# Attention and ELU feed-forward on one Trainium2 core: the first tile's scores put ahead of the global queries' scores and fetched first in pieces, the exponential table loaded at the start, and the weight conversion passes given lower priority while attention runs alone

## The chip, the core and the metric

The kernel runs on 1 core of one Trainium2 chip. The core has five engines with instruction queues of their own: TensorE (PE; its weight loads are shown apart as PEld), VectorE (DVE), ScalarE (ACT), GpSimd (POOL) and SyncE (SP, which issues most DMAs). An engine works off its queue in order, and an instruction waits until what it needs from other engines or from DMAs has been signalled. The metric is the device time of one execution in microseconds (us), lower is better.

## The reference

```python
B, H, Sl, Sg, D = 8, 8, 512, 32, 64
k_all, v_all = concat([k_g, k_l]), concat([v_g, v_l])
out_g = softmax(q_g @ k_all.T / 8) @ v_all            # 32 global queries see everything
s_ll  = where(|i - j| <= 32, q_l @ k_l.T / 8, -1e9)   # local queries see a window ...
out_l = softmax(concat([q_l @ k_g.T / 8, s_ll])) @ v_all   # ... and the 32 global keys
x = concat([out_g, out_l]) as (4608, 512)
h = x @ w_in                                          # 512 -> 2048
out = where(h > 0, h, exp(min(h, 0)) - 1) @ w_out     # 2048 -> 512
```

Inputs and outputs are fp32. The weights arrive with their 64 bits as pairs of 32-bit words (`w_in`, `w_out` are doubles), so the kernel has to turn them into numbers that TensorE can take.

## The kernel before, in words

**Two streams of work share the engines.** One is attention, the other the feed-forward network (FFN). The program is written as Python generators that take turns; a tile framework then orders the instructions of each engine by priority (the place in the program, shifted by `high_priority`), and that order is fixed when the kernel is built.

**Attention** goes through slots. A slot `("g", b, g)` treats the global queries of four heads (batch b, head group g), a slot `("l", b, g, t)` one tile of 128 local queries of four heads. Stage S of a local slot (`stage_s`) computes four score tiles of 128x160 on PE (L769), then DVE adds the mask and takes the row extreme (L780), ACT takes the exponential (L786), DVE adds and inverts the sums (L790, L791, L795), and POOL scales (L793). Stage T transposes the four tiles on PE (L809), and DVE or ACT copies them back (L811). Stage U transposes the global part (L742, L744, L745; copies L746, L748, L750 on ACT, sum L753 on DVE). Stage V multiplies with the values (L853, L822), ACT copies the result (L859), DVE sums and takes the maximum (L864, L866, L868). The global slot (`stage_ga`) has its scores (L703, L706), maxima (L715, L716), exponentials (L720, L722), and `norm` (L726 to L728 on DVE; L731, L732 on POOL). Slots were listed for batch 0 as g, then four l, then g, four l.

**The alone stretch.** For the first 66 steps of attention (`PACE`), `lead[0]` is true: FFN work is not started. Only the weight conversion runs beside attention. `load_weights` works in units: unit 0 is the first 256 columns of `w_in`, unit 1 the matching rows of `w_out`, unit 2 `w_in` again, and so on; two raw buffers (`raw`) alternate, so the fetch of unit 2 (SP, L174) has to wait until unit 0 has read its raw buffer for the last time. The passes of a unit are s0 (absolute value on ACT L188, clamp on POOL L189), s1a, s1b, s1c (three integer passes on DVE: L193, L196, L200), s1d (maximum on ACT, L204, which is the last user of `raw`), s2 (for `w_in` units the maximum over partitions, a PE transpose L141 and a DVE reduction L142), s3 (scale, high half on ACT L213) and s4 (low half on DVE L216). `tables` then makes group scales that the FFN needs.

**FFN.** A block of 256 tokens is split in high and low halves (`split_x`: L568 on ACT, L571 on DVE), multiplied on PE (L324), put through ELU (ACT L333, L334, L335, L349; DVE L342, L345) and multiplied again (L447, later L482 in a form with seven products). In PE's queue the first FFN product stands behind a dozen tiles' attention work.

**Start.** Ten PE products of zeros (`WARM`, L152) run first. The queue of SP begins with the global queries, two k tiles of 640 KB, two q tiles of 256 KB, the mask of 240 KB, then weights and values.

## Time and profile before

| | |
|---|---|
| median of 3 runs | 953.43 us (948.69, 953.43, 953.65) |
| profiled execution | 954.72 us, span of the trace 952.9 us |
| granted TensorE clock, mean | 0.977 |
| PE busy | 908.5 us (95%) |
| DVE busy | 728.1 us (76%) |
| ACT busy | 670.1 us (70%) |
| POOL busy | 271.1 us (28%) |
| first attention score product (L769) starts | 7.89 us |
| first exponential of a score tile (L786) starts | 11.23 us |
| first FFN product (L324) starts | 77.15 us |

Times in the trace count from the span's start. A row of the timeline reads: start, duration, engine, line, operation, what is written and read, the shape, the number of like instructions merged, and in brackets the idle time of that engine before it and what ended it. A row of the windows view gives for one stretch the busy time of each engine, the granted clock of PE, the busy share of the DMA engines and GB/s.

### The profile page before, as it was taken

Reading aid. Unit: us, or ns where it says so; the run is one execution under the profiler, and the core shown is the slowest. Engines: PE = TensorE matmul, PEld = TensorE weight load, DVE = VectorE, ACT = ScalarE, POOL = GpSimd, SP = SyncE. Lnnn points to the kernel's source line nnn. Section 1 sums busy time; section 2 is a strip of 40 time slices with the busy share of each in tenths; the row PEclk is TensorE's granted clock in tenths of the full one; section 3 lists DMA queues with packets and bytes.
Section 4 is the critical chain, followed back from the end, with each engine's and each line's share of the span. In section 5 each row is a group of like instructions: output and inputs, shape, how many; then the busy total and the mean of one; then the engine's idle time right before and its main releaser. Section 6 shows DMA issues by size and latency. Waiting matters only on the chain.

```text
span 952.9 us, 23830 instructions
## 1 busy us (share of the span) xinstructions
PE 908.5 (95%) x9216; PEld 727.8 (76%) x9216; DVE 728.1 (76%) x2025; ACT 670.1 (70%) x1584; POOL 271.1 (28%) x483
## 2 busy tenths in 40 slices
PE   6889887899999999999999999999999999999997
PEld 3567564566666788888888888888888888888886
DVE  4988988889967777768776877687777777676566
ACT  5888996776656767757677767677767767666564
POOL 4655481461522322122121212221332312100000
PEclk8779999899999999999999999999999999999999
DMA  6855876331342023101330123102310101000000
GB/s 262 299 179 180 282 224 191 124 123 57 115 157 90 23 100 103 47 26 46 105 121 26 46 78 125 47 27 79 122 49 25 46 23 35 2 23 23 1 24 23
DMA packets 41769, 87.64 MB, mean 92 GB/s; under 512 B 7736, under 2 KB 8888, under 8 KB 41656
## 3 DMA queue, kind: packets, MB, share of 16 engines
q1 hardware_dynamic: 41368, 85.85, 26.6%
q8 instruction: 73, 1.20, 0.5%
q14 instruction: 40, 0.33, 0.1%
q10 hardware_dynamic: 288, 0.26, 0.1%
HBM read 70.89 MB, written 15.20 MB: 90 GB/s over the span
## 4 chain that ended last, share of the span: by engine, by line
PE 67%; DVE 14%; ACT 9%; POOL 3%; issue 3%; DMA 3%; SPq 0%; DVEq 0%; ACTq 0%; POOLq 0%
PE pa L324 25%; PE acc L482 12%; PE h L482 9%; PE acc L447 4%; PE pa L822 3%; PE h L324 3%; PE pa L769 3%; PE pa L809 2%; ACT p L786 2%; DMA raw<-w_out 2%; PE pa L889 2%; DVE gl L345 1%; POOL p L793 1%; DVE cu L196 1%; DVE cu L200 1%
## 5 line engine op out<-in xcount | busy, mean ns | idle before, releaser
L324 PEld LDWEIGHTS <-winh 128*128 128x128 f16 x2160 | 209.4, 98 | 39.2 <-issue 8.4
L793 POOL TENSOR_SCALAR p<-p,sm 128x128 f32<-128x128 f32 x256 | 147.8, 593 | 303.2 <-DVE sm L791 165.0
L324 PE MATMUL pa<-xh,winh 128*128 128x256 f16 x824 | 224.9, 273 | 0.1
L324 PE MATMUL pa<-xl,winh 128*128 128x256 f16 x824 | 224.6, 273 | 0.0
L324 PE MATMUL pa<-xh,winl 128*128 128x256 f16 x824 | 224.6, 273 | 0.0
L361 ACT ACTIVATE gh<-gx,xs 128x896 f16<-128x896 f32 x103 | 107.3, 1042 | 123.1 <-DVE gx L358 123.0
L345 DVE SCALAR_TENSOR_TENSOR gl<-gx,xs,gh 128x896 f16<-128x896 f32 x103 | 119.4, 1159 | 59.9 <-ACT gh L361 59.0
L482 PEld LDWEIGHTS <-gh 128*128 128x128 f16 x1456 | 139.5, 98 | 24.0 <-issue 7.4
L786 ACT ACTIVATE p<-p,m 128x160 f32<-128x160 f32 x256 | 106.7, 421 | 41.6 <-DVE m L780 41.4
L324 PEld LDWEIGHTS <-winl 128*128 128x128 f16 x1080 | 106.1, 98 | 14.3 <-issue 1.2
L333 ACT ACTIVATE g<-pa,xs 128x512 f32<-128x512 f32 x103 | 70.3, 682 | 24.4 <-PE pa L324 23.8
L482 PE MATMUL acc<-wouth,gh 128*128 128x256 f16 x312 | 85.2, 273 | 0.0
L482 PE MATMUL acc<-woutl,gh 128*128 128x256 f16 x312 | 85.1, 273 | 0.0
L335 ACT ACTIVATE g<-g 128x512 f32<-128x512 f32 x135 | 85.0, 630 | 0.1
L482 PE MATMUL acc<-wouth,gl 128*128 128x256 f16 x312 | 85.0, 273 | 0.0
L482 PEld LDWEIGHTS <-gl 128*128 128x128 f16 x728 | 71.2, 98 | 9.2 <-DVE gl L345 1.0
L482 PE MATMUL h<-raw,gh 128*128 128x256 f16 x416 | 75.0, 273 | 0.0
L324 PE MATMUL h<-xh,winh 128*128 128x256 f16 x256 | 71.1, 279 | 1.5 <-ACT hs L334 0.9
L324 PE MATMUL h<-xl,winh 128*128 128x256 f16 x256 | 71.0, 278 | 0.7 <-DVE xl L571 0.7
L324 PE MATMUL h<-xh,winl 128*128 128x256 f16 x256 | 71.0, 278 | 0.0
L780 DVE CUSTOM_DVE_ANT_0 p<-pa,msk 128x160 f32<-128x160 f32 x228 | 61.5, 318 | 4.8 <-PE pa L769 4.7
L342 DVE SCALAR_TENSOR_TENSOR gx<-g,hs 128x512 f32<-128x512 f32 x51 | 35.9, 704 | 36.0 <-ACT g L335 35.6
(236 smaller groups left out, 2016.9 us busy)
## 6 DMA issues: line engine op xcount, KB each, us to landing
k<-kT SPq DMA_DIRECT2D x32, 640.0 KB, 5.1
v<-vT SPq DMA_DIRECT2D x64, 256.0 KB, 2.8
q<-qT SPq DMA_DIRECT2D x32, 256.0 KB, 5.6
raw<-w_in SPq DMA_DIRECT2D x8, 1024.0 KB, 5.9
raw<-w_out SPq DMA_DIRECT2D x8, 1024.0 KB, 6.8
out<-o SPq DMA_DIRECT2D x32, 256.0 KB, 2.3
od<-o SPq DMA_DIRECT2D x24, 256.0 KB, 3.1
o<-od SPq DMA_DIRECT2D x24, 256.0 KB, 2.8
```

The source lines that it names most:

```text
L324: nc.tensor.matmul(h[:, j, :], wt[:, c, f], xt[:, c, :], start=k == 0, stop=k == 11)
L333: nc.scalar.activation(g, hf, AF.Relu, scale=sc[:, p:p + 1])
L335: nc.scalar.activation(g, g, AF.Exp, scale=-1.0)
L342: nc.vector.scalar_tensor_tensor(out=out, in0=ins[0], scalar=-1.0, in1=ins[1], op0=ALU.add, op1=ALU.max)
L345: nc.vector.scalar_tensor_tensor(out=dst, in0=src, scalar=sg, in1=hi, op0=ALU.mult, op1=ALU.subtract)
L361: nc.scalar.activation(gh, gx, AF.Copy, scale=sg)
L447: nc.tensor.matmul(acc[t], gt[:, s], wt[:, f, :], start=p == first and j == 0 and k == 0, stop=p == last and j == 1 and k == 2)
L482: nc.tensor.matmul(cols, gt, w, start=p == 0 and k == 0, stop=last and k == len(todo) - 1, skip_group_check=True)
L769: nc.tensor.matmul(sp[r][half * HQ:(half + 1) * HQ, j * KW:(j + 1) * KW], q[rows, qs], k[rows, t, half, :], start=True, stop=True)
L780: nc.vector.tensor_tensor_reduce(out=p, in0=sp[r][:, j * KW:(j + 1) * KW], in1=msk[:, mi, :], op0=ALU.add, op1=ALU.min, scale=-scale, scal ...
L786: nc.scalar.activation(ps[i], ps[i], AF.Exp, bias=m[:, i:i + 1], scale=-1.0, accum_out=s[:, 0, i:i + 1])
L793: nc.gpsimd.tensor_scalar(ps[i][:, 0:P], ps[i][:, 0:P], s[:, 1, i:i + 1], 1.0, ALU.mult, ALU.mult)
```

## The change

Seven edits, all in the start and the alone stretch:

1. The slots of batch 0 begin with the first local tile; the first global slot comes second.
2. `first_loads` replaces the two calls of `loads`: SP fetches the keys of tile 0 (`k[:, 0]`, 160 KB each), ACT's queue the queries of tile 0 (64 KB each), SP the first third of the mask (80 KB), then the global queries, the rest of k, the rest of q, the rest of the mask.
3. A tile `early` of one column is set to zero and put through `Exp` at the start.
4. `WARM` goes from 10 to 8.
5. In the alone stretch the passes s1a, s1b, s1c, s1d, s3 and s4 of a unit get a priority 60 places lower (`behind`); s0 and s2 keep theirs.
6. `behind` moves from `add_up` to the top, unchanged.
7. The mask is no longer fetched in `loads`.

```diff
-WARM = 10
+WARM = 8
...
+    def behind(fn):
+        with tc.high_priority(offset=-BEHIND):
+            fn()
...
+    early = wts.tile([P, 1], F32, name="early")
+    nc.vector.memset(early, 0.0)
+    nc.scalar.activation(early, early, AF.Exp)
...
-            defer(i, fn)
+            defer(i, (lambda fn=fn: behind(fn)) if lead[0] and fn not in (s0, s2) else fn)
...
-                slots += [(*a, *t) for g in range(2) for a, t in [(("g", b, g), ())] + [(("l", b, g), (t,)) for t in range(NT)]]
+                slots += [("l", b, 0, 0), ("g", b, 0)] + [("l", b, 0, t) for t in range(1, NT)]
+                slots += [("g", b, 1)] + [("l", b, 1, t) for t in range(NT)]
...
-                if i == 1:
-                    nc.sync.dma_start(msk, mask)
-
-        for i in range(AHEAD):
-            loads(i)
+
+        def first_loads():
+
+            st = sts[0]
+            for hp in range(2):
+                k = st["k", hp] = apool.tile([P, NT, 2, KW], F32, name="k", bufs=4)
+                q = st["q", hp] = apool.tile([P, SL], F32, name="q", bufs=4)
+                nc.sync.dma_start(k[:, 0], kT[0, hp][:, 0])
+                nc.scalar.dma_start(q[:, 0:P], qT[0, hp][:, 0:P])
+            nc.sync.dma_start(msk[:, 0, :], mask[:, 0, :])
+            st["qg", 0] = load_qg(0, 0)
+            for hp in range(2):
+                nc.sync.dma_start(st["k", hp][:, 1:], kT[0, hp][:, 1:])
+            for hp in range(2):
+                nc.sync.dma_start(st["q", hp][:, P:], qT[0, hp][:, P:])
+            nc.sync.dma_start(msk[:, 1:, :], mask[:, 1:, :])
+
+        first_loads()
```

How the built queues differ. In the rows of the change line numbers are 3 to 7 higher (L786 is now L789, L188 now L195, L204 now L211, L174 now L181, L780 now L783, L141 now L145, L216 now L223).

ACT, from its first instruction, before (`pg`, `pu` are the global queries' exponentials, `p_94`, `p_95`, `p_93` the score tiles of the first three local tiles, `cu` a conversion unit):

```order
L720 ACT_TABLE_LOAD
L720 ACTIVATE pg,sg<-pa,mg 128x4x64 x2
L722 ACTIVATE pu,sg<-pa,mg 128x32
L786 ACTIVATE p_94,sm<-p_94,m 128x160 x4
L188 ACTIVATE cu<-raw 128x1024
L786 ACTIVATE p_95,sm<-p_95,m 128x160 x4
L786 ACTIVATE p_93,sm<-p_93,m 128x160 x2
L188 ACTIVATE cu<-raw 128x1024
```

and in the change:

```order
L947 DMA q<-qT 128x128 x2
L157 ACT_TABLE_LOAD
L157 ACTIVATE early<-early 128x1
L789 ACTIVATE p_94,sm<-p_94,m 128x160 x4
L723 ACTIVATE pg,sg<-pa,mg 128x4x64 x2
L725 ACTIVATE pu,sg<-pa,mg 128x32
L789 ACTIVATE p_95,sm<-p_95,m 128x160 x4
L789 ACTIVATE p_93,sm<-p_93,m 128x160 x2
L195 ACTIVATE cu<-raw 128x1024
```

The table load stands at the head, the first tile's exponentials ahead of the global ones, and the first absolute value behind ten exponentials where it was behind four.

DVE, around the first tile of the second head group (`p_95` here), before: the three integer passes of unit 2 (L193, L196, L200) stand ahead of its scores.

```order
L193 TENSOR_SCALAR cu<-cu 128x1024
L216 SCALAR_TENSOR_TENSOR winl<-cu,cm,winh 128x4x256
L196 SCALAR_TENSOR_TENSOR cu<-raw,cu 128x1024
L726 TENSOR_REDUCE sg<-sg 128x1
L866 TENSOR_TENSOR xglob<-xglob,h 128x2x32
L200 SCALAR_TENSOR_TENSOR cu<-raw,cu 128x1024
L727 TENSOR_SCALAR sg<-sg 128x1
L868 TENSOR_REDUCE xm<-xr 128x1
L728 RECIPROCAL sg<-sg 128x1
L780 ISA p_95,m<-acc,msk 128x160
```

and in the change, from the same sum of the global queries to the end of that tile's scores and the pass behind them:

```order
L729 TENSOR_REDUCE sg<-sg 128x1
L730 TENSOR_SCALAR sg<-sg 128x1
L731 RECIPROCAL sg<-sg 128x1
L200 TENSOR_SCALAR cu<-cu 128x1024
L223 SCALAR_TENSOR_TENSOR woutl<-cu,cm,wouth 128x1024
L223 SCALAR_TENSOR_TENSOR winl<-cu,cm,winh 128x4x256
L783 ISA p_95,m<-acc,msk 128x160
```

Two of the three integer passes of unit 2 have moved behind this tile's scores; both low halves (L216, now L223) of units 0 and 1 stand right ahead of them.

PE, the second tile's transposes, before and in the change (`cm` is the maximum of weight unit 0):

```order
L822 MATMUL h<-ptw_81,v 64x96 x4
L141 MATMUL pa<-ident,cm 128x128
L809 MATMUL pa<-ident,p_95 128x128 x4
L742 MATMUL pa<-ident,pz 128x128
L745 MATMUL pa<-ident,pg 128x128
```

```order
L825 MATMUL h<-ptw_81,v 64x96 x4
L145 MATMUL pa<-ident,cm 128x128
L812 MATMUL pa<-ident,p_95 128x128 x4
L745 MATMUL pa<-ident,pz 128x128
L748 MATMUL pa<-ident,pg 128x128
```

Nothing moved here: in both, the second tile's transposes stand behind the maximum of unit 0, whose last pass is one of those that got the lower priority.

The queues differ only at their beginning. Line numbers and buffer numbers aside, the last difference stands at place 625 of PE's 12,309 entries, 358 of DVE's 1,997, 156 of ACT's 1,067, 72 of POOL's 242 and 53 of SP's 174.

## The prediction

> **What bounds the kernel now.** First I read the page's slices for PE and its clock, to see where time can be won at all.

> ```profile
> PE   6889887899999999999999999999999999999997
> PEclk8779999899999999999999999999999999999999
> ```

> After the first eight slices (190 us) PE is nine tenths busy or more at full clock. A stretch table by what the change touches says more; its columns are length, then busy time and count for PE, PEld, DVE, ACT, POOL, then clock, DMA share, GB/s.

> ```profile
> 0.00:9.06 9.06, 7.49 (x63) 3.41 (x66) 1.33 (x4) 0.30 (x1) 2.69 (x12) 1.00 0.76 274
> 9.06:22.79 13.73, 6.20 (x53) 3.60 (x48) 9.13 (x41) 11.67 (x40) 6.35 (x12) 0.73 0.71 273
> 22.79:36.97 14.18, 11.89 (x148) 8.53 (x144) 13.03 (x42) 10.40 (x30) 8.11 (x13) 0.90 0.77 269
> 36.97:62.48 25.51, 24.07 (x266) 16.69 (x262) 22.47 (x112) 21.25 (x78) 16.80 (x32) 0.73 0.80 270
> 62.48:77.15 14.67, 11.52 (x124) 8.43 (x117) 11.20 (x48) 10.54 (x37) 10.85 (x31) 0.77 0.27 82
> 77.15:135.00 57.85, 52.73 (x502) 37.32 (x500) 50.83 (x148) 53.76 (x128) 33.61 (x51) 1.00 0.71 241
> 200.00:952.90 752.90, 740.39 (x7701) 615.86 (x7699) 564.44 (x1508) 511.60 (x1177) 166.24 (x295) 1.00 0.18 61
> ```

> From 200 us PE works 740.39 of 752.90 us; nothing there is touched, all queues being the same from about 135 us on. So what is won or lost before is carried to the end, and the question is how much earlier the state at 135 us comes. Until the first FFN product at 77.15 us DVE has the fullest row: idle 7.73, 4.60, 1.15, 3.04 and 3.47 us in the five stretches (length less busy), 20.0 in all. The same DVE work stands ahead of that product before and after (four units up to s1c, four low halves, the same tiles), so its start moves by the idle time that goes or comes. That is my bookkeeping. The waits behind the idle time, from the timelines:

> ```profile
> 1.18 4.21 PE L152 MATMUL acc<-wouth 128*128 128x512 f16 x10 [1.18 <-DVE wouth L150]
> 6.84 0.63 PE L703 MATMUL pa<-k,qg 64*32 64x256 f32 x4 [0.39 <-DMA k<-kT]
> 7.89 0.50 PE L769 MATMUL acc<-k,q 64*64 64x160 f32 x8
> 9.06 0.33 DVE L780 CUSTOM_DVE_ANT_0 p<-acc,msk 128x160 f32<-128x160 f32 x1 [0.38 <-PE acc L769]
> 8.76 1.28 ACT L720 ACT_TABLE_LOAD   x1 [8.76 <-DVE mg L716]
> 10.06 0.47 ACT L720 ACTIVATE pg<-pa,mg 128x256 f32<-128x256 f32 x1
> 11.23 0.43 ACT L786 ACTIVATE p<-p,m 128x160 f32<-128x160 f32 x1
> 11.64 0.42 ACT L786 ACTIVATE p<-p,m 128x160 f32<-128x160 f32 x1
> 12.36 1.37 POOL L731 TENSOR_SCALAR pk<-pu,sg 32x32 f32<-32x32 f32 x4 [8.90 <-ACT p L786]
> 13.82 0.70 POOL L732 TENSOR_SCALAR pg<-pg,sg 128x512 f32<-128x512 f32 x1
> 14.93 1.17 PE L809 MATMUL pa<-ident,p 128*128 128x128 f32 x3 [3.89 <-POOL p L793]
> 16.72 0.69 DVE L193 TENSOR_SCALAR cu<-cu 128x1024 int32<-128x1024 int32 x1 [2.86 <-POOL cu L189]
> 18.77 0.27 ACT L750 COPY ptg<-pa 128x128 f32<-128x128 f32 x1
> 18.83 1.22 DVE L196 SCALAR_TENSOR_TENSOR cu<-raw,cu 128x1024 int32<-128x1024 int32 x1
> 21.53 1.16 ACT L204 ACTIVATE raw<-cu 128x1024 f32<-128x1024 f32 x1 [0.53 <-DVE cu L200]
> 22.42 0.80 PE L853 MATMUL h<-ptg,ptw 128*64 128x160 f32 x4 [2.98 <-DVE ptg L753]
> 22.79 0.38 SPq L174 DMA_DIRECT2D raw<-w_in  x1
> 24.96 0.48 PE L141 MATMUL pa<-ident,cm 128*128 128x128 f32 x1
> 36.97 0.30 DVE L780 CUSTOM_DVE_ANT_0 p<-acc,msk 128x160 f32<-128x160 f32 x1
> ```

> and from the waits of SP's queue (total, times, longest):

> ```profile
> SPq L174 <- ACT raw L204: 22.4, 5, 11.1
> ```

> To be seen: the first exponential of a tile comes at 11.23 us, behind a table load of 1.28 us that waits 8.76 us for the global maxima, and behind the global exponentials. POOL gets its first attention work at 12.36, the transposes start at 14.93, the values only at 22.42. SP holds the third weight fetch, and all loads queued behind it, for 11.1 us until L204 of unit 0 ends, and issues it at 22.79. The second tile's transposes stand behind L141 at 24.96, which waits for the same L204.

> **The change part by part.** *Start.* Eight warm products end at 1.18 + 8 x 0.42 = 4.55 us. The small pieces are 528 KB; at the 274 GB/s of the first stretch that is 1.9 us, and bytes flow from about 2 us on, so they land by about 4. The score products then start at 4.6, and DVE's first score row follows as before by 9.06 - 7.89 = 1.17, at 5.7 us: 3.3 us earlier. The first exponential follows at about 6.0, 5.2 us earlier. The two warm products less cost nothing here: PE would wait for data anyway. The table load lies in ACT's idle 8.76 us, behind two DMA issues like SP's of 0.38 us (from about 0.7: 0.7 + 0.8 + 1.28 = 2.8, well before 6.0). If that cover were gone it would cost the 1.28 us of its row. The memset and the one-column exponential cost DVE and ACT some 0.2 us each, in idle time too.

> The global scores now need the rest of k, fetched third; up to it 1.5 MB have to land, where the second k tile (1.3 MB with the first) landed at 6.84 with 0.75 MB on the way beside it, so about 7 us, and DVE waits for them from 6.2 to 7.7. SP issues nine transfers ahead of the first weights where it issued six, 3 x 0.4 = 1.2 us more; their reader L188 moves back behind ten exponentials (10 x 0.41 us) and starts at about 12.7 as against 12.88, so the later landing stays hidden, narrowly.

> *First tiles.* DVE then does sums of tile 0 and the second tile's scores (to 10.5); POOL scales tile 0 from about 8.8, and the transposes start at 9 (14.93 before). POOL's global scaling (1.37 + 0.70) follows at 11.3 and ends at 13.4; three ACT copies of 0.27 us behind the transposes end at 14.6, and the first values start at 15.0 as against 22.42, 7.4 us earlier. The lowered passes of unit 0 go behind that: clamp on POOL to 15.8, the DVE passes 0.69 + 1.22 + 1.22 us from there to 19.0, with small sums in their overlaps, L204 to about 20.4. So SP's hold opens 2.4 us earlier, and L141 comes at 20.5, 4.4 us earlier. DVE's idle time up to there: 4.8 (start), 1.65 (rest of k), 0.35 and 0.1 (global exponentials), 1.0 (copies), 0.95 (clamp), 8.85 in all, against 12.33 in the first two stretches: **3.5 us won**.

> *Middle.* The order behind gives some of it back. ACT's absolute value of unit 2 now stands between the global exponentials and their last one, so DVE's L726 waits for it. By the same sums over in-order queues I find three DVE waits: 1.4 us at 20 (the clamp of unit 1 stands behind POOL's scaling of the third tile), 2.6 at 27.4 (L726, behind two copies' groups, 1.0 of global exponentials and L188's 1.13 on ACT) and 0.6 at 30 (the clamp of unit 2): 4.6 in all, where the stretch from 22.79 to 36.97 has 1.15, so 3.45 more. The scores of the second head group start near 33.7 (36.97 before), but two passes of 1.22 us that stood ahead of them now follow. I may set POOL and ACT too late, as each is less full than DVE there: I take **2.5 us lost**, between 0 and 3.45. The stretch from 36.97 to 62.48 I leave at its 3.04 us of idle time: lowered passes may fill part of it (up to 3.0 won), and new waits may come.

> *End of the alone stretch.* Here one stall in ACT's queue is moved past.

> ```profile
> 64.60 1.13 ACT L188 ACTIVATE cu<-raw 128x1024 f32<-128x1024 f32 x1 [1.61 <-DMA raw<-w_out]
> 65.63 1.13 ACT L568 ACTIVATE xh<-xr,xm 128x1024 f16<-128x1024 f32 x1
> 66.79 2.14 DVE L571 SCALAR_TENSOR_TENSOR xl<-xr,xm,xh 128x1024 f16<-128x1024 f32 x1 [1.52 <-ACT xh L568]
> 67.82 1.08 PE L809 MATMUL pa<-ident,p 128*128 128x128 f32 x4 [2.41 <-ACT pg L720]
> 70.51 0.80 PE L853 MATMUL h<-ptg,ptw 128*64 128x160 f32 x4
> 73.58 0.23 DVE L864 COPY xglob<-h 128x64 f32<-128x64 f32 x1 [1.51 <-ACT xr L859]
> ```

> L188 waits 1.61 us for weights while L568 and the global exponentials stand behind it; DVE idles 1.52, PE 2.41, its clock falls (0.77 in this stretch), the values at 70.51 take long, and DVE idles another 1.51. In the change's queue L568 stands ahead of that L188, and between them two exponentials, three copies and another exponential. The first 1.52 goes, and of the second, which hangs on the clock, I count 1.0: **2.5 us won**, between 0 (the wait only changes its victim, since the global exponentials still stand behind L188) and 3.47, the stretch's whole idle time.

> *From 77 to 135 us* DVE is 50.83 and ACT 53.76 of 57.85 us busy with the same work in nearly the same order: carried, 0 +- 1.5.

> Sum: 3.5 - 2.5 + 2.5 = 3.5 us won. Against the profiled execution's own time, 954.72, that is 951.2; this execution lies 1.3 above the median 953.43 of the runs shown, so the forecast is **949.9 us**.

> [...]

> **The rivals.** *A, given back.* The DVE passes are the real bound: all three waits come in the middle and the stall at L188 only changes its victim. For it: DVE's row from 22.79 to 62.48 is 35.5 of 39.7 us busy. Against it: attention runs ahead, so passes have other work beside them. 3.5 - 3.45 + 0 = 0: 953.4 us.

> *B, carried whole.* The attention chain bounds, not DVE: no wait is lost in the middle and the last stretch loses its idle time. For it: the values come 7.4 us and L141 4.4 us earlier, and DVE is idle for 20.0 us in all. Against it: the shared L204. 3.5 + 0 + 3.5 = 7.0: 946.4 us.

> *C, the clock.* PE is idle 3.89 us before 14.93, and the table gives clock 0.73 behind it. In the change PE has little between the first values (done at about 16.3) and L141 at 20.5, 4.2 us, so the spell of low clock moves into the second tile's transposes, the second values and the global scores. One group of values takes

> ```profile
> 23.01 0.85 PE L822 MATMUL h<-ptw,v 128*64 128x96 f32 x8
> 30.78 0.50 PE L822 MATMUL h<-ptw,v 128*64 128x96 f32 x8
> ```

> 0.85 us slow and 0.50 fast; the four groups of a tile 2.6 and 1.3. Two tiles of values and as much again for transposes and scores cost 2 x 1.3 + 1 = 3.6 us where PE's queue is waited for: the gain is gone, 953.5 us. [...]

> *D, slower.* L141 in PE's queue is the place. It stands unmoved ahead of the second tile while L204, for which it waits, is lowered. If unit 0's passes slip behind one more tile (the ten exponentials, POOL's scaling of two tiles, DVE's scores of two), L204 ends at about 28 instead of 22.8, and the second tile, the global slot and all loads behind SP's third weight fetch come 5.2 us later; the later stall then stays as it is. 953.43 + 5.2 = 958.6 us. It decides as soon as L204 of unit 0 ends after 22.8. Against it: I find 20.4.

> That the change does not do what it says is no rival: the queues show that it does.

> **How the numbers follow.** Forecast 949.9: 0.37 (its own range 948 to 952). A 953.4: 0.20. B 946.4: 0.27. C 953.5: 0.08. D 958.6: 0.08. About 0.5% (4.8 us) is what a measurement of this kernel can tell from no change; the three runs shown differ by 5. Faster by more than that means below 948.7: B, and a third of the forecast, 0.39. Slower means above 958.2: most of D, 0.07. The rest, 0.54, is within. The range reaches to B's time with 2 us more won in the middle, 944.5, and on the other side past A and C, with 2 us for the spread of runs, to 955.5.

> **What would show it.** First score row on DVE near 5.7 us, first exponential near 6.0, first values near 15, L204 of unit 0 ending near 20.4, the scores of the second head group near 33.7, no wait of ACT ahead of L568, first FFN product near 73.6 us (77.15 less 3.5), and PE's row behind 200 us as before. DVE's idle time ahead of the first FFN product should be 16.5 us. The prediction is wrong if L204 of unit 0 ends after 22.8 (D), if DVE idles 20 us again (A), or if the first FFN product comes earlier but the gain is gone at 135 us.

## The result, and the profile after

The change takes 957.49 us (median of 7 runs, 956.36 to 958.24), the kernel before in the same session 952.08 (7 runs, 948.69 to 953.65): ratio 1.0061, 95% interval 1.0042 to 1.0081, so slower by 0.6%. Measured a second time beside later experiments it was 956.18 (10 runs), ratio 1.0068 (1.0047 to 1.0088). Forecast were 949.9 us and a range up to 955.5. One execution of a kernel differs from the next by several microseconds (948.69 to 953.65 for the kernel before; PE's slices of half clock fall differently, as shown below, in its second trace 1 to 8 us elsewhere than in the first), so single traces are compared with that in mind.

The profiled execution took 958.24 us with a span of 956.4 us (before 954.72 and 952.9). The stretch table over the prediction's stretches (length, busy time and count of PE, PEld, DVE, ACT, POOL, then clock, DMA share, GB/s):

```profile
0.00:9.06 9.06, 6.72 (x47) 2.98 (x48) 1.35 (x10) 3.24 (x10) 2.69 (x12) 1.00 0.78 246
9.06:22.79 13.73, 7.15 (x83) 4.87 (x79) 10.15 (x47) 10.21 (x37) 8.54 (x19) 0.75 0.74 292
22.79:36.97 14.18, 11.77 (x120) 7.64 (x122) 10.39 (x29) 8.88 (x24) 7.79 (x9) 0.88 0.82 276
36.97:62.48 25.51, 18.65 (x224) 13.23 (x224) 24.03 (x98) 20.50 (x70) 14.05 (x26) 0.87 0.77 252
62.48:77.15 14.67, 10.06 (x160) 7.38 (x158) 13.25 (x74) 12.51 (x47) 12.73 (x34) 1.00 0.34 108
77.15:135.00 57.85, 52.72 (x484) 37.11 (x484) 48.04 (x133) 49.53 (x119) 28.90 (x45) 0.94 0.66 224
```

DVE's idle time (length less busy) is now 7.71, 3.58, 3.79, 1.48 and 1.42 us in the first five stretches, 17.98 in all: 2.0 us less than the 19.99 before. PE moved the other way: it was busy 24.07 and 11.52 us in the fourth and fifth stretch and is now busy 18.65 and 10.06, in part because its clock is higher there (0.87 and 1.00, before 0.73 and 0.77). The start, from the timelines:

```profile
6.08 0.33 DVE L783 CUSTOM_DVE_ANT_0 p<-acc,msk 128x160 f32<-128x160 f32 x1 [4.95 <-PE acc L772]
9.06 0.46 DVE L718 TENSOR_REDUCE mg<-pa 128x1 f32<-128x288 f32 x1 [1.92 <-PE pa L709]
9.44 0.16 DVE L793 TENSOR_SCALAR sm<-sm 128x4 f32<-128x4 f32 x1
10.20 1.46 POOL L796 TENSOR_SCALAR p<-p,sm 128x128 f32<-128x128 f32 x4 [6.74 <-DVE mg L719]
11.44 0.63 PE L812 MATMUL pa<-ident,p 128*128 128x128 f32 x4 [1.03 <-POOL p L796]
13.06 1.36 POOL L734 TENSOR_SCALAR pk<-pu,sg 32x32 f32<-32x32 f32 x4 [1.40 <-DVE sg L731]
16.15 0.33 DVE L783 CUSTOM_DVE_ANT_0 p<-pa,msk 128x160 f32<-128x160 f32 x1 [1.96 <-PE pa L772]
17.13 0.29 DVE L756 TENSOR_REDUCE ptg<-pa 128x32 f32<-128x128 f32 x1
17.47 0.80 PE L856 MATMUL h<-ptg,ptw 128*64 128x160 f32 x4 [1.47 <-DVE ptg L756]
20.54 0.23 DVE L867 COPY xglob<-h 128x64 f32<-128x64 f32 x1 [0.75 <-ACT xr L862]
20.68 1.34 DVE L207 SCALAR_TENSOR_TENSOR cu<-raw,cu 128x1024 int32<-128x1024 int32 x1
22.05 1.14 ACT L211 ACTIVATE raw<-cu 128x1024 f32<-128x1024 f32 x1
23.33 0.48 PE L145 MATMUL pa<-ident,cm 128*128 128x128 f32 x1 [3.24 <-ACT raw L211]
```

The first score row comes 2.98 us earlier than before, but the tile's sums (L793) stand in DVE's queue behind the global maxima (L718), and those wait for the rest of k until 9.06. The lead is 3.5 us at the transposes and 5.0 at the first values (22.42 before), and in this trace it is gone at the last pass of unit 0 on ACT: L211 starts at 22.05, before 21.53. In the two other traces of the change, told of further down, it starts at 22.93 and 20.86 (before 21.66 and 21.63).

Behind that PE has a wait that is far longer than in the kernel before. The rows of DVE and PE in the change:

```profile
38.77 1.28 DVE L203 SCALAR_TENSOR_TENSOR cu<-raw,cu 128x1024 int32<-128x1024 int32 x1
40.61 1.21 DVE L207 SCALAR_TENSOR_TENSOR cu<-raw,cu 128x1024 int32<-128x1024 int32 x1
41.74 0.68 DVE L814 COPY ptw<-pa 128x512 f32<-128x512 f32 x1
42.48 0.91 PE L825 MATMUL h<-ptw,v 128*64 128x96 f32 x8 [3.02 <-DVE ptw L814]
```

and in the kernel before:

```profile
38.83 0.68 DVE L811 COPY ptw<-pa 128x512 f32<-128x512 f32 x1
39.57 0.91 PE L822 MATMUL h<-ptw,v 128*64 128x96 f32 x8 [0.74 <-DVE ptw L811]
```

The two passes of unit 2 that moved behind the fifth tile's scores now stand ahead of the fourth tile's copy, and PE waits 3.02 us for it where it waited 0.74. All three traces of the change show 3.02 or 3.03 us here, all three of the kernel before 0.74. The fifth tile's transposes then start at 44.38, 45.72 and 43.16 us, before at 41.55, 41.70 and 41.93: 2.7 us late on the mean.

The end of the alone stretch and the place of the second slice of half clock:

```profile
62.34 0.79 PE L772 MATMUL pa<-k,q 64*64 64x160 f32 x16 [1.54 <-ACT ptg L753]
68.42 0.32 PE L145 MATMUL pa<-ident,xm 128*128 128x128 f32 x1 [2.05 <-DVE ptw L814]
72.05 1.31 DVE L574 SCALAR_TENSOR_TENSOR xl<-xr,xm,xh 128x1024 f16<-128x1024 f32 x1 [0.37 <-ACT xh L571]
72.09 2.41 POOL L734 TENSOR_SCALAR pk<-pu,sg 32x32 f32<-32x32 f32 x4
73.45 0.44 PE L856 MATMUL h<-ptg,ptw 128*64 128x128 f32 x4 [1.05 <-ACT ptg L753]
76.06 2.83 POOL L796 TENSOR_SCALAR p<-p,sm 128x128 f32<-128x128 f32 x8
76.49 1.54 PE L812 MATMUL pa<-ident,p 128*128 128x128 f32 x4 [1.30 <-POOL p L796]
78.47 0.42 PE L327 MATMUL h<-xh,winh 128*128 128x256 f16 x1
105.08 0.58 PE L450 MATMUL acc<-wouth,gh 128*128 128x512 f16 x1 [1.60 <-DVE o L458]
```

The first FFN product starts at 78.47 us, 1.32 later than before. It takes 0.42 us where the same product took 0.27 before: PE runs at half clock here (granted clock 0.50 from 77.44 to 80.85 us), and again at 105 us (0.50 from 104.75 to 108.16). The wait of ACT for `raw<-w_out` ahead of the split is gone, as forecast; the last wait ahead of the product is now PE's for POOL.

**One account holds for all 20 traces.** Take as second mark the first ELU step that reads its products from the `pa` banks (ACT, L333 before, L336 now): 313.33 us before, 316.46 now. From the first FFN product to this mark PE executes the same 1895 matmuls; in the change some of those between the 228th and the 447th come in another order. The stretch is 214.0 us (213.4 to 214.3 over the 20 traces) plus PE's idle time in it plus half of its busy time at half clock in it; after the mark 639.5 to 640.1 us follow. The rows, the first from the start to the first FFN product, the second from there to the mark; of the kernel before:

```profile
0.00:77.15 77.15, 61.16 (x631) 40.67 (x632) 57.16 (x243) 54.15 (x181) 44.80 (x98) 0.80 0.67 235
77.15:313.33 236.18, 218.39 (x1895) 147.65 (x1893) 202.37 (x498) 179.64 (x411) 98.81 (x145) 0.98 0.46 153
```

and of the change:

```profile
0.00:78.47 78.47, 55.59 (x629) 37.08 (x630) 59.68 (x254) 56.09 (x190) 47.12 (x101) 0.88 0.68 231
78.47:316.46 237.99, 221.15 (x1894) 148.76 (x1893) 200.47 (x487) 177.93 (x403) 95.55 (x143) 0.97 0.45 152
```

So the 3.56 us between the two spans are: 1.32 up to the first FFN product; 2.76 more PE busy time for the same products (the clock was at half for 16.0 us of this stretch against 10.2); 0.94 less idle time (16.84 against 17.79); 0.4 behind the mark.

### The profile page after: what moved, and what is told of

The parts are those of the page before. It is cut to its first block, busy times and chain, and to the rows that moved or that the text cites. A ratio compares the mean times of both kernels' runs of the same rounds, so it can differ in the third digit from the quotient of the medians.

```text
span 956.4 us, 23843 instructions
## 1 busy us (share of the span) xinstructions
PE 905.9 (95%) x9214; PEld 725.6 (76%) x9214; DVE 729.5 (76%) x2026; ACT 670.7 (70%) x1585; POOL 266.8 (28%) x483
## 4 chain that ended last, share of the span: by engine, by line
PE 70%; DVE 13%; ACT 9%; issue 3%; POOL 2%; DMA 2%; SPq 0%; DVEq 0%; POOLq 0%; ACTq 0%
PE pa L327 25%; PE acc L485 12%; PE h L485 9%; PE acc L450 5%; PE h L327 4%; PE pa L825 4%; PE pa L772 3%; PE pa L812 2%; PE pa L892 2%; ACT p L789 2%; PE pa L706 1%; DVE gl L348 1%; DMA k<-kT 1%; DVE cu L203 1%; DMA raw<-w_out 1%
## 5 line engine op out<-in xcount | busy, mean ns | idle before, releaser
L796 POOL TENSOR_SCALAR p<-p,sm 128x128 f32<-128x128 f32 x256 | 138.4, 558 | 317.2 <-DVE sm L794 172.6
L789 ACT ACTIVATE p<-p,m 128x160 f32<-128x160 f32 x256 | 106.7, 420 | 45.8 <-DVE m L783 43.1
L336 ACT ACTIVATE g<-pa,xs 128x512 f32<-128x512 f32 x103 | 70.3, 683 | 23.9 <-PE pa L327 23.3
L783 DVE CUSTOM_DVE_ANT_0 p<-pa,msk 128x160 f32<-128x160 f32 x228 | 61.0, 318 | 8.8 <-PE pa L772 8.5
L345 DVE SCALAR_TENSOR_TENSOR gx<-g,hs 128x512 f32<-128x512 f32 x51 | 35.9, 704 | 35.5 <-ACT g L338 35.1
```

Of the source, the lines that this page charges most:

```text
L336: nc.scalar.activation(g, hf, AF.Relu, scale=sc[:, p:p + 1])
L345: nc.vector.scalar_tensor_tensor(out=out, in0=ins[0], scalar=-1.0, in1=ins[1], op0=ALU.add, op1=ALU.max)
L783: nc.vector.tensor_tensor_reduce(out=p, in0=sp[r][:, j * KW:(j + 1) * KW], in1=msk[:, mi, :], op0=ALU.add, op1=ALU.min, scale=-scale, scal ...
L789: nc.scalar.activation(ps[i], ps[i], AF.Exp, bias=m[:, i:i + 1], scale=-1.0, accum_out=s[:, 0, i:i + 1])
L796: nc.gpsimd.tensor_scalar(ps[i][:, 0:P], ps[i][:, 0:P], s[:, 1, i:i + 1], 1.0, ALU.mult, ALU.mult)
```

## The experiments

Ratios are to the kernel before on the same chip, with the 95% interval; "product" is the start of the first FFN product, "idle" PE's idle time ahead of it, "half" the time at half clock between it and the mark, all in us of the profiled execution. The runs were made on several chips, on which the kernel before took 949.2 to 952.1 us, so the ratios are compared and not the times.

| run | us | ratio | product | idle | half |
|---|---|---|---|---|---|
| before (3 traces) | 952.08 | 1 | 77.15, 75.50, 75.65 | 16.0, 17.2, 16.4 | 10.2, 10.2, 6.8 |
| change (3 traces) | 957.49 | 1.0061 | 78.47, 79.41, 77.48 | 22.9, 23.0, 23.2 | 16.0, 10.2, 12.4 |
| no lowering | 955.63 | 1.0058 (1.0035 to 1.0081) | 78.97 | 22.6 | 6.8 |
| lowering alone | 954.44 | 1.0043 (1.0028 to 1.0059) | 75.31 | 21.7 | 10.2 |
| unit 0 kept | 953.62 | 1.0038 (1.0020 to 1.0055) | 79.77 | 21.6 | 10.2 |
| only s3, s4 low | 955.29 | 1.0056 (1.0037 to 1.0074) | 80.71 | 19.4 | 10.2 |
| only s1a to s1d low | 957.89 | 1.0077 (1.0048 to 1.0105) | 81.97 | 21.5 | 17.1 |
| before, PE filled | 952.32 | 1.0005 (0.9982 to 1.0028) | 77.94 | 10.4 | 13.7 |
| change, PE filled | 951.75 | 1.0013 (0.9996 to 1.0031) | 75.51 | 11.3 | 10.2 |
| change, end filled | 954.21 | 1.0042 (1.0026 to 1.0058) | 78.11 | 20.3 | 6.8 |
| change, L145 later | 959.23 | 1.0086 (1.0058 to 1.0114) | 83.10 | 20.1 | 17.1 |
| before, later maxima | 961.28 | 1.0112 (1.0079 to 1.0144) | 77.42 | 17.5 | 17.1 |
| early table alone | 951.25 | 1.0009 (0.9987 to 1.0032) | 78.96 | 20.3 | 6.8 |
| pieces, old order | 954.96 | 1.0048 (1.0024 to 1.0072) | 77.72 | 20.5 | 13.7 |
| slot order alone | 959.27 | 1.0082 (1.0051 to 1.0114) | 83.26 | 22.0 | 13.7 |
| lowering, table, end filled | 951.13 | 1.0011 (0.9992 to 1.0030) | 77.88 | 18.9 | 6.8 |

**Which part costs.** First the lowering was taken out, and put in alone:

```diff
-            defer(i, (lambda fn=fn: behind(fn)) if lead[0] and fn not in (s0, s2) else fn)
+            defer(i, fn)
```

> The change with edit 5 undone: all passes of the conversion keep their priority; slot order, first fetches in pieces, early table and WARM 8 stay. Theory L (the lowered passes are what costs): the 5.4 us of the change against the kernel before come from them, and the start alone wins some of the 3.5 us forecast; 948 to 951 us, the first FFN product before 77.15 us. Rival S (the start costs: pieces, nine transfers ahead of the weights, first absolute value behind ten exponentials): the time stays with the change, 956 to 958 us. Rival C (a spell of low clock meets the first FFN products and costs 1.2 us in the change): it is a matter of where PE is idle, so the result would lie between, 954 to 956.

> The kernel before with edit 5 alone. Theory L: 955 to 958 us, L204 of unit 0 later than 22.8 us and the later low halves bunched ahead of the first FFN product, which comes after 77.15. Rival S: 950 to 952 us, no slower than before.

Without the lowering the change is as slow (1.0058), and the lowering alone is slow too (1.0043): both theories fall in their simple form, and the two losses do not add up. The traced execution of the lowering alone, 950.47 us, is the fastest of its 12, and its span of 948.5 us is that of a trace of the kernel before; so where its 0.43% goes no trace shows. In the run without lowering unit 0's L211 starts at 22.03 us and the second tile's transposes at 23.57, in the change at 22.05 and 23.60. So the late maximum of unit 0 comes from the start edits, not from the lowered passes. The fifth tile's transposes are late without the lowering as well (45.17 us), but behind other waits: 2.46 us at 35.63 and 1.44 at 43.04, both for a copy on ACT.

Then two kinds of passes, and unit 0, were kept out of the lowering. Of these lines one stands in each of the three kernels:

```diff
-            ... if lead[0] and fn not in (s0, s2) else fn)
+            ... if lead[0] and (m or p) and fn not in (s0, s2) else fn)
+            ... if lead[0] and fn in (s3, s4) else fn)
+            ... if lead[0] and fn in (s1a, s1b, s1c, s1d) else fn)
```

> The change, but the passes of weight unit 0 keep their priority; all later units are lowered as in the change. If the loss is made at L145 (PE idle for 3.24 us ahead of 23.33 us, waiting for the maximum of unit 0), the maximum comes about 3 us earlier and most of the loss goes: 953 to 955 us. If it is made by the later units (their maxima, scales and low halves queue up between 40 and 78 us), the time stays at 956 to 958 us although L145 comes earlier.

> The change, but only s3 and s4 (scale with high half, low half) are lowered; the integer passes and the maximum (s1a to s1d) keep their priority. If the lowered integer passes cost (they hold up the maxima and with them PE's L145 and the next weight fetch): 950 to 953 us. If the lowered scales and low halves cost: 956 to 958 us as the change.

> The change, with only the integer passes and the maximum (s1a to s1d) lowered; s3 and s4 keep their priority. The counterpart of the run with only s3 and s4 lowered, which was 0.56% slower than before. If lowered scales and low halves cost: near the kernel before, 950 to 952 us. If any lowering costs nothing beside the start edits: 955 to 957 us.

None is as fast as the kernel before; the intervals overlap with the change's, and all three have the first FFN product later than the change. In the first the maximum of unit 0 did not come earlier either (L211 at 23.07). No single group of lowered passes is the cause.

**The place of L145 (rival D).** The maximum of unit 0 was put behind the second tile's transposes; its scale, its low half and the tables of the first group move back with it:

```diff
-        lag = 7 if m else 16
+        lag = 7 if m else (16 if m or p else 18)
...
-                defer(12, lambda group=group: tables(group))
+                defer(12 + 2 * (group == "a"), lambda group=group: tables(group))
```

> The change, with the maximum of weight unit 0 over partitions (s2, L145), s3 and s4 two steps later and the tables of group a two steps later, so that L145 stands behind the second tile's transposes in PE's queue and not ahead of them. If PE's 3.24 us idle at L145 is what costs (rival D of the prediction): the second tile's transposes near 21.5 instead of 23.6 to 24.5 us, the time 953 to 954 us. If the place of L145 does not matter because the third tile waits for POOL and the later loads for the raw buffers anyway: 956 to 957 us.

PE's timeline of that run:

```profile
16.22 1.11 PE L812 MATMUL pa<-ident,p 128*128 128x128 f32 x4
24.21 0.48 PE L145 MATMUL pa<-ident,cm 128*128 128x128 f32 x1
```

The second tile's transposes came 7.4 us earlier, and the kernel became slower (1.0086), its first FFN product 4.6 us later. The wait at L145 is real, and taking it away in this way buys nothing; what the passes that move with it cost by themselves was not measured. Nor does a similar move behind the alone stretch, in the kernel before:

```diff
-            defer(i, fn)
+            defer(i, (lambda fn=fn: behind(fn)) if not lead[0] and fn is s2 else fn)
```

with 200 places for `BEHIND` (which also lowers `add_up`, far behind, so that this is no clean measure):

> The kernel before, with the maxima over partitions of the units behind the alone stretch (s2) 200 places lower in priority. In both kernels PE waits 3.4 us near 156 to 164 us for such a maximum (L141 behind the last pass on ACT), and a slice of half clock follows where the wait fills a slice. If PE's queue is held there: 2 to 5 us faster than before. If ACT, which waits for the same weights, holds the ELU behind it too: within 1 us of before.

It was the slowest of all (1.0112); the reason was not followed up and stays open.

**Is a gain at the start carried?** The early table alone:

```diff
+    early = wts.tile([P, 1], F32, name="early")
+    nc.vector.memset(early, 0.0)
+    nc.scalar.activation(early, early, AF.Exp)
```

> The kernel before with edit 3 alone: the exponential table is loaded at the start. By the prediction's step the 1.28 us load leaves the way from the global maxima (8.76 us) to the first exponential: first exponential of a score tile at about 9.9 instead of 11.23 us. If the start is carried: 1.0 to 1.3 us faster than before, first FFN product earlier by as much. If the start is not carried (later waits take it): same within 1 us, the first FFN product at 75.5 to 77 us as in the two traces of before.

ACT's timeline there:

```profile
0.72 1.28 ACT L153 ACT_TABLE_LOAD   x1 [0.72 <-PEq L1067]
2.02 0.20 ACT L153 ACTIVATE early<-early 128x1 f32<-128x1 f32 x1
10.02 0.43 ACT L789 ACTIVATE p<-p,m 128x160 f32<-128x160 f32 x1
```

The first exponential of a score tile moved from 11.23 to 10.02, the transposes from 14.93 to 13.82 and unit 0's last pass on ACT from 21.53 to 20.36: 1.1 to 1.2 us each. But PE's first values start at 22.59 (22.42 before), behind 5.33 us of idle time: the sum on DVE that they need, L756 at 22.25, stands behind an integer pass that waits for POOL until 21.64. The time is the same (1.0009). So in this trace the lead at the start is gone on PE within 9 us. The first FFN product comes at 78.96 us, later than in any trace of the kernel before, and later than the 75.5 to 77 that I had expected; behind it PE idles 14.8 us and does 6.0 us of work at half clock, and the span, 950.4, lies among those of the kernel before (948.5 to 952.9). A late first product is thus no loss by itself. The slot order and the fetches in pieces apart (the first run is the change with edits 1 and 5 undone, the second the kernel before with edit 1 and the mask fetched one slot earlier, since the first slot is now a local one):

```diff
-                if i == 1:
+                if i == 0:
                     nc.sync.dma_start(msk, mask)
```

> The change without edits 1 and 5: first fetches in pieces, early table, WARM 8, but the slot order of before (the global queries first) and no lowering. If the slot order is what makes the first FFN product late in the change (78.5 and 79.4 us; 79.0 with no lowering): 75.5 to 77 us here, the time near before, 949 to 951 us. If the fetches in pieces with nine transfers ahead of the weights do it: 78 us or more, 953 to 956 us.

> The kernel before with edit 1 alone (the first local tile ahead of the global queries; queries and mask are then fetched ahead of the keys, since fetches follow the slots). If the slot order makes the first FFN product late: 78 us or more and 0.3 to 0.6% slower than before. If not: within 0.2% of before.

Both are slower. Pieces without the new order (with the early table and eight warm products) cost about what the start edits cost together (1.0048 and 1.0058). The order alone has its first score row at 11.85 us, since its keys are fetched behind queries and mask, so that it is no clean measure of the order.

**More traces of both kernels.** The traces of one kernel differ, and the account says in what:

> The kernel before, unchanged, for a second trace of it. Theory G (the granted clock is set in slices of about 3.41 us, in traces so far every spell of half clock is a multiple of that, and where the slices fall differs from one execution to the next): the spells lie elsewhere than at 15.3, 39.2, 66.5, 162.0 and 182.5 us, and the time from the first FFN product to the first group product of the later form (313.33 us less 77.15, 236.2) differs by 1 to 3 us with the low slices in it. Rival: the spells belong to the kernel and come at the same times within 1 us, and the distance is 236.2 again.

> The change, unchanged, for a second trace. Theory G: the first FFN product comes near 78.5 us again (its lateness of 1.3 us against the kernel before is the kernel's own) within 1 us, but the spells of low clock behind it (77.4, 104.7, 166.2 and 186.7 us) move or are fewer, and the span is up to 4 us shorter. Rival: same spells and same span of 956.4 within 1 us.

> The kernel before, unchanged, for a third trace. Account A, found in all 18 traces so far: from the first FFN product to the first group product of the later form the time is 214.0 us (213.4 to 214.3) plus PE's idle time there plus half of PE's busy time at half clock there, and 639.5 to 640.1 us follow. So the span has to be the time of the first FFN product, that idle time and that half, plus 853.6, within 0.6. Theory M (the two traces of before at hand, 952.9 and 950.6 us, came from its slower executions; its median on the later chips is 949.2 to 950.7): span near 948, the three terms together near 94.5 us, where they were 99.2 and 97.1. Rival: the terms are 97 to 99 again, and the medians differ from the traces for another reason.

> The change, unchanged, for a third trace. By account A its span is 854 us plus the three terms, which were 102.7 and 98.5 us. If the change's loss lies in these terms: near 100 to 101 us, the first FFN product at 78.4 to 79.5 us with PE idle 22 to 24 us ahead of it (16.0 and 17.2 in the kernel before), and a slice of half clock starting within 3 us of that product. Rival: the first FFN product below 77.5 us.

The third trace of the kernel before:

```profile
0.00:75.65 75.65, 59.24 (x631) 38.94 (x631) 56.86 (x245) 53.98 (x181) 45.76 (x98) 0.84 0.69 240
75.65:308.94 233.29, 216.64 (x1895) 146.97 (x1893) 202.19 (x495) 179.67 (x410) 100.19 (x145) 0.99 0.47 155
```

and of the change:

```profile
0.00:77.48 77.48, 54.27 (x628) 36.03 (x629) 58.71 (x254) 56.05 (x190) 47.79 (x101) 0.90 0.68 234
77.48:311.48 234.00, 219.65 (x1894) 148.12 (x1893) 200.57 (x487) 177.89 (x403) 95.85 (x143) 0.97 0.47 155
```

The account fits both spans: 75.65 + 16.65 + 2.6 + 853.6 = 948.5 and 77.48 + 14.35 + 5.55 + 854 = 951.4; measured 948.5 and 951.5. For the kernel before the three terms are 94.9 us, as theory M had it. For the change they are 97.4, where I had expected 100 to 101, and the product at 77.48 lies on the rival's side of 77.5; the idle time ahead of it, 23.2, and the slice of half clock beside it came as expected. In the second trace of the kernel before the spells lie 1 to 8 us elsewhere than in the first, but the distance to the mark, 235.5 us, differs by 0.7 only. Up to the first tiles the traces of one kernel differ by a microsecond or two, and then each wait comes again, shifted: in the second trace of the change the waits of PE listed above come at 63.65, 69.72, 74.75 and 77.81 us. The mean of three traces each:

| mean of three traces, us | before | change |
|---|---|---|
| first FFN product | 76.1 | 78.5 |
| PE idle from there to the mark | 17.1 | 15.1 |
| half of PE's busy time at half clock there | 3.8 | 5.9 |
| span | 950.7 | 953.6 |

The difference of the spans, 2.9 us, is 2.4 - 2.0 + 2.1 + 0.4 (behind the mark). The medians differ by more (5.4, and 5.9 the second time). The traced executions of before took 954.72, 952.45 and 950.81 us, two of them above all its medians (949.2 to 952.1); those of the change 958.24, 954.59 and 953.26, two of them below its 956.2 and 957.5. The traces thus explain about half of the timed difference; that the rest lies in the same three terms is likely, since everything else is constant within 1 us in 20 traces, but not shown.

All three traces of the change have a slice of half clock that begins within 1.3 us of the first FFN product, and one that begins 26 to 27 us behind it; none of the three of the kernel before has either.

**Holding the clock.** Four products of zeros were put ahead of each tile's transposes, and of each maximum, while attention runs alone; the transposes then overwrite the bank:

```diff
+HOLD = 4
...
+    def hold(tp):
+        for _ in range(HOLD if lead[0] else 0):
+            nc.tensor.matmul(tp, warm[:, 0:P], warm, start=True, stop=True)
...
+        hold(tp)
```

> The kernel before with four zero products of 128x512 on PE ahead of each transposed tile and each maximum while attention runs alone, written to the bank that the transposes then overwrite: PE's idle time is filled, so that its clock stays high there. If the low clock (30.7 of the first 77 us) lies on the path: the first FFN product 1 to 3 us earlier, and 1 to 3 us faster than before. If DVE's and ACT's queues bound the stretch: same within 1 us, or slower by the 0.9 us products where PE is waited for.

> The change with the same filling products. If the clock is what costs in the change (its first FFN products run at half clock for 2.3 us, the second tile behind L145 too): at or below the kernel before, and close to the same edit of the kernel before. If the lowered passes and the late weights cost: still 0.4 to 0.6% above the same edit of the kernel before.

On the kernel before the filling does nothing (1.0005). On the change it takes back nearly the whole loss (1.0013 where the change has 1.0061 and 1.0068; the intervals do not meet). PE's rows of the filled change:

```profile
0.00:75.51 75.51, 64.22 (x697) 38.93 (x698) 58.92 (x253) 55.32 (x187) 47.44 (x99) 0.98 0.69 241
75.51:308.30 232.79, 218.39 (x1895) 148.50 (x1893) 201.30 (x488) 178.60 (x409) 101.32 (x145) 0.98 0.46 155
```

Clock 0.98 ahead of the first FFN product where the change had 0.88, and that product 2 to 4 us earlier. The gain lies there and not behind it: between the product and the mark the clock is at half for 10.2 us, as in the second trace of the change. The filling also moved some instructions (L145 behind the second tile's transposes, which by itself was no gain), so it is not the clock alone that changed. Filling before the last three tiles only:

```diff
+            for _ in range(4 if lead[0] and n >= 8 else 0):
+                nc.tensor.matmul(tp, warm[:, 0:P], warm, start=True, stop=True)
```

> The change, with four zero products of 128x512 on PE ahead of the transposes of the last three tiles of the alone stretch only; the rest of the queue is the change's. Theory E (a spell of half clock at the first FFN products, seen at 77.4 and 79.3 us in both traces of the change and in neither of the kernel before, costs 1.2 to 1.7 us): 953.5 to 955 us, no spell at the first FFN product. Rival: PE's own products delay the last tiles, or the spell costs nothing since DVE bounds there: 956 to 957 us.

PE's timeline of it and the row from the product to the mark:

```profile
75.48 1.04 PE L812 MATMUL pa<-wouth 128*128 128x512 f16 x4
78.11 0.27 PE L327 MATMUL h<-xh,winh 128*128 128x256 f16 x1
```

```profile
78.11:310.01 231.90, 216.93 (x1895) 147.27 (x1893) 201.09 (x487) 178.20 (x405) 99.40 (x145) 0.99 0.47 156
```

The zero products stand where PE waited for POOL; the first FFN product comes no earlier, but takes 0.27 us, and neither of the two slices of half clock is there. Its time, 954.21, is 2 to 3 us below the change's (1.0042 against 1.0068 and 1.0061, with overlapping intervals). With the lowering and the early table on the kernel before, the same filling gives:

> The kernel before with the lowering (edit 5), the early table (edit 3) and four zero products on PE ahead of each of the last three tiles of the alone stretch. The lowering alone had its first FFN product at 75.3 us, against 77.15 and 75.5 of before, but a spell of half clock right there, and was 0.43% slower. If that spell is what made it slower: 2 to 4 us less than the lowering alone, 949 to 952 us, near before or under it. If the lowering costs otherwise: 953 to 955 us.

1.0011 where the lowering alone had 1.0043 (the intervals just touch), and the slice at the first FFN product is gone. That fits a cost of the lowering through the clock behind it, but does not show it, as no slow execution of the lowering alone was traced. No kernel tried here is faster than the one before.

## Why the prediction was wrong, step by step

**"So what is won or lost before is carried to the end"** and its bookkeeping, "the same DVE work stands ahead of that product before and after, so its start moves by the idle time that goes or comes": this is the step that failed. DVE did 254 instructions and 59.68 us of work ahead of the first FFN product where it had done 243 and 57.16: eleven more, ten of them most of a further tile of attention (a copy, the sums, three of four score rows), the last the memset of `early`. In the first pair of traces DVE's idle time ahead of the product shrank from 19.99 to 18.79 us, and 2.52 more work less 1.20 idle time is the 1.32 us by which the product came later. On the mean of three traces each the idle time is 19.2 and 19.1, so none of the forecast 3.5 us was won; the work is 56.9 and 59.4, and these 2.4 us are what the product is late. In-order queues had fixed the order on each engine, not how far DVE runs ahead of PE. The late product is in turn partly paid back as less idle time of PE behind it (2.0 of 2.4 us on the mean of three traces), so the bookkeeping was right neither for the product nor for the end.

Its premise was a wrong reading of the table, too: "DVE has the fullest row" until that product does not hold, since PE's five rows add up to 61.2 us and DVE's to 57.2. Part of PE's time was at half clock (30.7 of the 77.15 us, mean clock 0.80), but PE's waits should have been counted beside DVE's.

**Start, +3.5.** By its own measure (DVE's idle time in the first two stretches) 12.33 became 11.29: 1.0 won. The first rows were right (score row 6.08 for 5.7, exponential 6.45 for 6.0). "The transposes start at 9" was wrong, they start at 11.44: I let POOL scale tile 0 from 8.8, and the tile's sums stood behind the global maxima in DVE's queue, so that POOL began at 10.20. From there the values came at 17.47 for 15.0 and L204 of unit 0 ended at 23.28 for 20.4; the last part of that, L207 behind L867 at 20.54, hangs on values at half clock (17.47 us, in a stretch with granted clock 0.50 from 16.00 to 26.24). The early table alone then showed that even a gain of 1.2 us in the chain up to unit 0's last pass is not carried by PE.

**Middle, -2.5.** Right in size, in part by luck: the idle time from 22.79 to 36.97 us went from 1.15 to 3.79, 2.64 lost. The rows are

```profile
28.82 0.84 DVE L718 TENSOR_REDUCE mg<-pa 128x1 f32<-128x288 f32 x2 [1.29 <-PE pa L709]
32.21 1.14 ACT L195 ACTIVATE cu<-raw 128x1024 f32<-128x1024 f32 x1
33.66 0.15 DVE L729 TENSOR_REDUCE sg<-sg 128x1 f32<-128x3 f32 x1 [1.47 <-ACT pu L725]
```

The wait that I expected at L726 (now L729), behind the absolute value of unit 2, is there with 1.47 us at 33.66; I had given it 2.6 us at 27.4. The 1.29 us at L718, for scores on PE, I had not foreseen. "The second head group's scores near 33.7" became 37.59 with the start's lead gone.

**36.97 to 62.48 us, left as it was:** 1.56 us of DVE's idle time went (3.04 to 1.48), within the 3.0 that I allowed. By DVE's idle time this stretch was a gain, and here PE lost most against the kernel before: 3.02 us of waiting at 42.48, for 0.74. I had seen that "two passes of 1.22 us that stood ahead of them now follow" the scores, and gave it no price of its own.

**End, +2.5.** 3.47 became 1.42, 2.05 won, and ACT no longer waits for weights ahead of the split. But PE does: 1.54, 2.05, 1.05 and 1.30 us in the rows above. The last one hangs on POOL, where the first of four small L734 ran beside DVE's L574 and took 1.34 us; the group took 2.41 where it had taken 1.36. I had asked what DVE waits for and not what PE, the engine whose product is the mark, waits for next.

**"From 77 to 135 us: carried, 0 +- 1.5".** The 481st product of PE starts 57.0, 57.6 and 56.9 us behind the first in the three traces of the change, 54.6, 54.5 and 54.5 in those of the kernel before: 2.6 us lost on the mean. It is PE's clock: PE idles 5.0 to 5.1 us there in all six, and half of its busy time at half clock is 2.5 to 3.4 us in the change and nothing before. Up to the mark 1.81 us of the first pair remain; behind it the carry holds within 0.5 us.

**The rivals.** D (958.6 us) is nearest to the 957.49 measured, and that is luck. Its condition was met in the first trace (L204 of unit 0, now L211, ended at 23.28, after 22.8), but by 0.5 us and not by 5.2; in the third trace it was not met (22.06), and PE idled 23.2 us ahead of the product all the same. The lowering had no part in it, the second tile's transposes started 1.6 us earlier, and moving L145 out of the way made the kernel slower. A (given back) was right that DVE's idle time stays as it was, by the mean of three traces, and wrong that the time then does. B is refuted: it needed 7 us less idle time. C had the right kind of cause and the wrong place: I put the spell into the second tile, where PE's queue has room again, and it did its harm at the first FFN products and at 105 us, where PE is the bound; for its 3.6 us the runs show 2.1 more up to the mark, on the mean of three traces.

Of the signs that I listed, D's (after 22.8) came in two of three traces without D's cause, and A's (20 us idle) nearly did, with 18.8 to 19.6; "the first FFN product comes earlier but the gain is gone at 135 us" did not, since it came later. No sign that I listed watched PE's waits, or its busy share in the last slice ahead of that product, and that is where the change is seen.

## What to carry to other kernels

Idle time of one engine is no ledger when that engine can run ahead of the one that sets the end: count instead the waits of the engine that bounds what follows, here PE, and compare both kernels at a mark where the same instruction of that engine starts. A pass moved out of the way of one tile stands in the way of another: ask which. Look at how busy a stretch that is bound elsewhere hands PE over: in the change's three traces PE was 53 to 61% busy in the slice of 3.41 us ahead of the one with the first FFN product, and that product took 0.42 us at half clock; in the kernel before it was 93 to 97% busy, and the product took 0.27. One trace a kernel is not enough for differences below 0.5%; three traces and the fixed account told what one could not.

## What the runs showed of the hardware

**Small instructions on POOL took longer beside some on DVE.** One L734 of 32x32 takes 0.28 to 0.29 us. In the first trace of the change, up to 75 us, the four that began while a low half or a split ran on DVE (L223 or L574, 1.29 to 1.31 us) took 1.16, 1.16, 1.36 and 1.34, and the one that began beside L200 (0.69 us) 0.79; the group of four at 34.57 us took 3.62, and so did the one at 35.90 us in the second trace. Before, the four L731 at 37.22 and at 69.69 us ran free of such instructions in 1.36 us each.

**The exponential followed the table load at once.** With the early table alone the load of 1.28 us at 0.72 us was followed by its exponential at 2.02, 0.02 us behind it; in the kernel before the load at 8.76 was followed by its exponential at 10.06, 0.02 us behind it too.
